# One load of query weights in two pieces, 16 partitions and then 112

## The chip, the core and the metric

The kernel runs on one core of a Trainium2 chip. The core has five engines with queues of their own: TensorE (PE, matmuls; its weight loads are listed as PEld), VectorE (DVE), ScalarE (ACT), GpSimd (POOL) and SyncE (SP, which here issues nearly all transfers). Sixteen DMA engines move data between the chip's memory (HBM) and the core's on-chip memory of 128 partitions. Engines and transfers tell each other by semaphores that work is done. The metric is the device time of one execution in microseconds (us).

## The reference

One token goes through attention over a cache of 65,536 positions and then a bilinear feed-forward block, all in fp32:

```
xn = layernorm(x)                              # x: 1 x 512
q  = xn @ wq                                   # 512 x 4096: 32 heads of 128, 4 for each of 8 cache heads
p  = softmax(q . k_cache / sqrt(128))          # k_cache, v_cache: 8 x 65536 x 128
h  = x + (p @ v_cache) @ wo
out = h + ((ln(h) @ w_gate) * (ln(h) @ w_up)) @ w_down     # F = 1792
```

The two caches are 537 MB of the 564.66 MB that the kernel reads.

## The kernel before

Everything large passes through two buffers, `kv[0]` and `kv[1]`, each 128 partitions x 16,384 fp32 (64 KiB for a partition, 8.39 MB in all). The host lays each operand out in blocks of that shape. The loads alternate between the buffers: first the query weights `wq` into `kv[1]` (line 118), then the first block of the cache into `kv[0]` (`even(0)`, line 142), then 63 more blocks (4 of keys, 4 of values for each of 8 heads), then `wo`, `gu` (gate and up weights) and `wd` (down weights), which are cut into two, three and six pieces. SP issues them all on one queue, in the order of the program. Before each load from the second cache block on, SP waits for the semaphore `free`, which VectorE raises when TensorE is done with the buffer. The input row `x` (`x_row`) is loaded from ACT's queue.

TensorE works on a block in 32 windows of 512 columns (`windows`, line 355), a matmul each, with the small operand `st` held as weights. It waits for the block's semaphore: `s_a0` for `kv[0]`, `s_b0` for `kv[1]`. A transfer raises its semaphore by 16 when all of it has landed, and a wait for 16 stands before the first window.

At the start, VectorE makes the layernorm of `x` (lines 168 to 180), TensorE turns it into columns (line 352), and VectorE copies these columns into `st` (line 209, `diagonal(0)`) and raises `qt`; with `qt` and `s_b0` TensorE starts the windows over `wq` (lines 434 to 437). When these are done (`kd`), VectorE raises `free`, and SP issues the second block of the cache. The tensor `q_all` that follows is used by all heads. The order on each queue is that of the code; nothing is rearranged.

Of the kernel before, what the change touches and what calls it, by code (L numbers as in the profile page):

```python
# [8 lines left out]
P = 128  # L9
D = 512  # L10
HKV, REP, DH = 8, 4, 128
SK = 65536
CK = 16384
NT = SK // CK
TPC = CK // P
KT = D // P
# [25 lines left out]
def body(nc, xr, kvd, wq, wo, gu, wd, out):  # L42
    pe_e, dve_e, act_e, pool_e, sp = nc.tensor, nc.vector, nc.scalar, nc.gpsimd, nc.sync

    def tile(name, *shape, align=32):
        return nc.alloc_sbuf_tensor(name, list(shape), F32, align_bytes=align).ap()
# [15 lines left out]
    kv = [tile(f"kv{i}", P, CK, align=1024) for i in range(2)]  # L62
# [22 lines left out]
    def sem(name):  # L85
        sems.append(nc.alloc_semaphore(name))
        return sems[-1]
# [8 lines left out]
    s_b0, s_b18, s_b28 = (sem(f"s_b{i}") for i in (0, 18, 28))  # L96
    s_wd = [sem(f"s_wd{i}") for i in WD_CUTS[:-1]]
    s_xr, s_wo = sem("s_xr"), sem("s_wo")
    late, s_act, s_pool, s_y, s_out = (sem(n) for n in ("late", "s_act", "s_pool", "s_y", "s_out"))
    wd_t = kv[0]  # L100
    end = 2 * HKV * NT

    def take(e, s, n=1):
        e.wait_ge(s, n).then_inc(s, -n)  # L104
# [10 lines left out]
    def odd(g):  # L115
        sp.dma_start(kv[1], kvd[g]).then_inc(s_b0, 16)

    sp.dma_start(kv[1], wq).then_inc(s_b0, 16)
    pe_e.br("pe_main")
    dve_e.br("dve_main")  # L120
    take(act_e, da)
# [74 lines left out]
    def diagonal(lo):  # L196
        return bass.AP(tensor=st.tensor, offset=33 * lo, ap=[list(st.ap[0]), [256, KT], [33, 8 - lo]])

    def spread(a, n):
        return a.unsqueeze(2).to_broadcast([P, KT, n])  # L200
# [5 lines left out]
        take(dve_e, pd)  # L206

    picked = ptp[0][:, 0:32].rearrange("p (b c) -> p b c", b=4)
    dve_e.tensor_copy(diagonal(0), spread(ps[0][:, 0:KT], 8)).then_inc(qt, 1)
    dve_e.sem_inc(tl, 1)  # L210
    take(dve_e, kd)
# [310 lines left out]
```

## Time and profile before

| | us |
|---|---|
| median of 3 runs | 1308.34 (1308.08 to 1308.45) |
| profiled execution, its own time | 1308.59 |
| its span, from the first to the last instruction | 1307.3 |
| TensorE busy in the span | 676.0 |
| VectorE busy | 102.9 |
| read from HBM | 564.66 MB |

The page gives busy times and, in 40 slices of the span, the busy share in tenths of each engine and of the 16 DMA engines. Views of the trace give the waits (who waited, for whom, how long in total, how often, the longest), the timeline (start, length, engine, line, operation, output <- inputs, count, and in brackets the idle time before and what ended it), windows (busy times, granted clock, DMA share and rate in a stretch) and the chain of waits that ended last. "SPq" is an issue by SP.

### The profile page before, as it was taken

The numbers are of one execution on the slowest core, as the hardware profiler recorded it, in microseconds if no ns is written. First come the engines' busy times: TensorE is split into PE (matmuls) and PEld (weight loads), VectorE is DVE, ScalarE is ACT, GpSimd is POOL, SyncE is SP. The second block draws the span as 40 slices with busy tenths as digits, with TensorE's granted clock in tenths as the row PEclk, the third lists the DMA queues.
The fourth block names the chain that finished last, engine by engine and source line by source line (L and its number), as shares of the span: only waits on it lengthen the run. The fifth ranks groups of instructions, "written<-read, shape, count | busy, mean of one in ns | idle before, by whom it ended". The sixth has DMA issues, their size and how long they took to land. (4 is left out here: it accounts for less than half of the span.)

```text
span 1307.3 us, 10815 instructions
## 1 busy us (share of the span) xinstructions
PE 676.0 (52%) x4606; PEld 187.8 (14%) x4606; DVE 102.9 (8%) x251; ACT 54.9 (4%) x106; POOL 4.2 (0%) x14
## 2 busy tenths in 40 slices
PE   3446445446535644554643654454563555355457
PEld 1112111111101111111110111111110111111112
DVE  2001010010000000000000101001000100000011
ACT  0000000000000000000000000000000000000000
POOL 1000000000000000000000000000000000000000
PEclk9676677677677767767667777867776776776779
DMA  9999999999999999999999999999999999999999
GB/s 417 417 449 417 449 417 449 417 449 419 447 435 431 439 427 449 417 449 417 449 417 449 417 449 419 447 435 431 441 425 449 417 449 417 449 417 449 417 433 387
DMA packets 11074, 564.72 MB, mean 432 GB/s; under 512 B 1233, under 2 KB 1345, under 8 KB 1858
## 3 DMA queue, kind: packets, MB, share of 16 engines
q1 hardware_dynamic: 11072, 564.72, 99.8%
q10 hardware_dynamic: 2, 0.00, 0.0%
HBM read 564.66 MB, written 0.06 MB: 432 GB/s over the span
## 5 line engine op out<-in xcount | busy, mean ns | idle before, releaser
L360 PE MATMUL ps<-kv,st 128*32 128x512 f32 x4308 | 620.2, 738 | 562.6 <-DMA kv<-in_kv 541.8
L360 PEld LDWEIGHTS ps<-kv,st 128*32 128x32 f32 x4308 | 150.0, 132 | 1016.5 <-DMA kv<-in_kv 586.1
L244 DVE TENSOR_REDUCE mx<-sc 128x1 f32<-128x512 f32 x32 | 22.0, 686 | 577.9 <-DVEq L104 577.9
L416 PE MATMUL ptp<-ident,ex 128*128 128x128 f32 x128 | 27.3, 371 | 19.8 <-ACT ex L226 19.5
L222 ACT COPY sc<-ps 128x512 f32<-128x512 f32 x32 | 18.7, 585 | 440.2 <-ACTq L104 440.1
L226 ACT ACTIVATE ex<-sc,nbias 128x512 f32<-128x512 f32 x32 | 22.8, 714 | 304.4 <-ACTq L104 304.4
L276 DVE TENSOR_TENSOR orow<-ps,orow 128x512 f32<-128x512 f32 x16 | 11.1, 692 | 261.6 <-DVEq L104 261.6
L222 ACT ACT_TABLE_LOAD x8 | 10.3, 1283 | 427.7 <-ACTq L104 427.7
L263 DVE COPY st<-ptp 128x512 f32<-128x512 f32 x32 | 22.1, 692 | 44.5 <-DVEq L104 44.5
L416 PEld LDWEIGHTS ptp<-ident,ex 128*128 128x128 f32 x128 | 20.2, 188 | 22.9 <-ACT ex L226 22.9
L409 PE MATMUL sm<-ident,m 128*1 128x128 f32 x16 | 4.5, 283 | 27.3 <-DVE m L246 17.6
L279 DVE TENSOR_TENSOR orow<-ps,orow 128x256 f32<-128x256 f32 x16 | 6.0, 420 | 138.5 <-DVEq L104 138.5
L274 DVE COPY orow<-ps 128x512 f32<-128x512 f32 x8 | 5.5, 692 | 101.7 <-DVEq L104 101.7
L411 PE MATMUL sm<-ones,mexp 1*128 1x1 f32 x32 | 6.9, 281 | 6.8 <-DVE mexp L253 6.8
L448 PE MATMUL ptp<-ident,orow 128*128 128x128 f32 x32 | 6.6, 293 | 3.0 <-DVE orow L279 3.0
L409 PEld LDWEIGHTS sm<-ident,m 128*1 128x1 f32 x16 | 1.3, 79 | 41.8 <-DVE m L246 24.9
L411 PEld LDWEIGHTS sm<-ones,mexp 1*128 1x128 f32 x32 | 5.5, 214 | 9.5 <-DVE mexp L253 8.5
L226 ACT ACTIVATION_READ_ACCUMULATOR ex<-sc,nbias 128x1 f32 x32 | 6.0, 186 | 0.0
L236 DVE COPY st<-qx 128x1024 f32<-128x1024 f32 x8 | 5.6, 694 | 1.2
L352 PE MATMUL ps<-ident,xn_row 1*128 1x1 f32 x4 | 0.6, 245 | 8.8 <-DVE xn_row L180 8.8
L205 DVE COPY gu_sb<-ps 128x256 f32<-128x256 f32 x4 | 1.5, 420 | 32.0 <-DVEq L104 32.0
L448 PEld LDWEIGHTS ptp<-ident,orow 128*128 128x128 f32 x32 | 3.2, 140 | 5.3 <-DVE orow L279 3.7
(78 smaller groups left out, 58.9 us busy)
## 6 DMA issues: line engine op xcount, KB each, us to landing
kv<-in_wo SPq DMA_DIRECT2D x1, 6144.0 KB, 24.2
kv<-in_gu SPq DMA_DIRECT2D x1, 3584.0 KB, 17.6
kv<-in_gu SPq DMA_DIRECT2D x1, 2560.0 KB, 23.3
kv<-in_wo SPq DMA_DIRECT2D x1, 2048.0 KB, 28.7
kv<-in_wd SPq DMA_DIRECT2D x2, 1024.0 KB, 15.4
kv<-in_kv SPq DMA_DIRECT2D x64, 29.0
kv<-in_gu SPq DMA_DIRECT2D x1, 1024.0 KB, 25.2
kv<-in_wd SPq DMA_DIRECT2D x2, 512.0 KB, 17.6
```

The source lines that it names most:

```text
L222: act_e.copy(sc[s], ps[s % 2]).then_inc(ad, 1)
L226: act_e.activation(ex[s - n], sc[s], AF.Exp, bias=nbias[:, 0:1], scale=SCALE, accum_out=sums[:, s:s + 1]).then_inc(atok[s - n], 1)
L236: dve_e.tensor_copy(st, qx.rearrange("p (g c) -> p g c", c=32)).then_inc(qt, 2)
L244: dve_e.tensor_reduce(out=mx[:, s:s + 1], in_=sc[s], axis=AX.X, op=ALU.max).then_inc(own, 1)
L263: dve_e.tensor_copy(st[:, :, 0:16].rearrange("p g (b h) -> p b g h", h=REP), ptp[n % 2].rearrange("p (b g h) -> p b g h", b=4, h=REP)).the ...
L276: mine(dve_e.tensor_tensor(out=orow, in0=ps[n % 2], in1=orow, op=ALU.add))
L279: dve_e.tensor_tensor(out=orow[:, cs], in0=ps[1][:, cs], in1=orow[:, cs], op=ALU.add).then_inc(tob, 1)
L360: i = mm(ps[buf][32 * j:32 * j + 32, :], st[:, 8 * j + r, :], kv[buf][:, w * 512:(w + 1) * 512], start=(r == 0), stop=(r in (1, 2, 7)), sk ...
L409: pe_e.transpose(sm[1][0:1, 0:P], m1, ident).then_inc(pd, 1)
L411: mm(sm[0][:, 0:1], mexp.rearrange("p g h -> p (g h)"), ones[0:1, 0:1], start=True, stop=True).then_inc(pd, 1)
L416: i = pe_e.transpose(ptp[half][:, b * P:(b + 1) * P], ex[half][:, b * P:(b + 1) * P], ident)
L448: i = pe_e.transpose(ptp[1][:, b * P:(b + 1) * P], orow[:, b * P:(b + 1) * P], ident)
```

## The change

The one load of `wq` becomes two. The first takes one row of 64 KiB into each of partitions 0 to 15 and has a semaphore of its own, `s_wq`. The second takes partitions 16 to 127 and raises `s_b0`, as the whole load did. The host lays the weights out as 16 pieces of 8 rows: the first row of piece e is that of partition e, the other seven are those of partitions 16+7e to 22+7e. The first load reads the first rows of the 16 pieces, the second the other seven of each. VectorE waits for `s_wq` before it copies the columns of the layernorm into `st`.

```
-    sp.dma_start(kv[1], wq).then_inc(s_b0, 16)
+    sp.dma_start(kv[1][0:16, :], wq[:, 0, :]).then_inc(s_wq, 16)
+    sp.dma_start(kv[1][16:P, :], wq[:, 1:8, :]).then_inc(s_b0, 16)
...
     picked = ptp[0][:, 0:32].rearrange("p (b c) -> p b c", b=4)
+    take(dve_e, s_wq, 16)
     dve_e.tensor_copy(diagonal(0), spread(ps[0][:, 0:KT], 8)).then_inc(qt, 1)
...
+    q = lay(A_wq, KT, P, HKV, 512, perm=(1, 2, 0, 3)).reshape(P, CK)
...
-        "wq": lay(A_wq, KT, P, HKV, 512, perm=(1, 2, 0, 3)).reshape(P, CK),
+        "wq": np.concatenate([q[0:16].reshape(16, 1, CK), q[16:P].reshape(16, 7, CK)], axis=1),
```

SP's queue at its start, before (`in_wq` and `in_kv` are the tensors in HBM; the sizes are partitions x elements):

```order
L118 DMA kv<-in_wq 128x16384
L113 DMA kv<-in_kv 128x16384
L143 UNCONDITIONAL_BRANCH
L116 ISA
L116 DMA kv<-in_kv 128x16384
```

and after:

```order
L118 DMA kv<-in_wq 16x16384
L119 DMA kv<-in_wq 112x1x16384
L113 DMA kv<-in_kv 128x16384
L144 UNCONDITIONAL_BRANCH
L116 ISA
L116 DMA kv<-in_kv 128x16384
```

The first cache block now stands third instead of second; nothing else of this queue moved.

VectorE's queue around the copy into `st`, with the semaphores that it waits for, before:

```order
L187 TENSOR_SCALAR neg_mean<-mean_m,sel 128x128 [waits own]
L191 COPY sel_pad<-sel 128x1 [waits pool]
L192 COPY acc<-x_row 1x512
L209 COPY st<-ps 128x4x8 [waits own,pd]
L205 COPY gu_sb<-ps 128x256 [waits kd]
```

and after:

```order
L188 TENSOR_SCALAR neg_mean<-mean_m,sel 128x128 [waits own]
L192 COPY sel_pad<-sel 128x1 [waits pool]
L193 COPY acc<-x_row 1x512
L211 COPY st<-ps 128x4x8 [waits own,pd,s_wq]
L206 COPY gu_sb<-ps 128x256 [waits kd]
```

The copy has one more wait, for the load of 16 partitions; its place is the same.

More of the change, by code (lines that the diff above doesn't have):

```diff
@@ L98, in body @@
     s_xr, s_wo = sem("s_xr"), sem("s_wo")
-    late, s_act, s_pool, s_y, s_out = (sem(n) for n in ("late", "s_act", "s_pool", "s_y", "s_out"))
+    late, s_act, s_pool, s_wq, s_y, s_out = (sem(n) for n in ("late", "s_act", "s_pool", "s_wq", "s_y", "s_out"))
     wd_t = kv[0]
```

## Prediction

> **What bounds the kernel now.** I read the page first, for the share of each engine and of the DMA engines.
>
> ```profile
> span 1307.3 us, 10815 instructions
> PE 676.0 (52%) x4606; PEld 187.8 (14%) x4606; DVE 102.9 (8%) x251; ACT 54.9 (4%) x106; POOL 4.2 (0%) x14
> DMA  9999999999999999999999999999999999999999
> DMA packets 11074, 564.72 MB, mean 432 GB/s; under 512 B 1233, under 2 KB 1345, under 8 KB 1858
> ```
>
> The busiest compute engine works for 52% of the span. The DMA engines are at 9 in all forty slices, the first and the last included: the transfer of 564.72 MB is the kernel. The tiny packets are worth a count. The program issues 77 transfers from SP (1 query weight, 64 cache, 2 `wo`, 3 `gu`, 6 `wd`, 1 output) and one small one from ACT; 77 x 16 + 1 = 1233, exactly the packets under 512 B. So each SP transfer ends with one tiny packet on each of 16 engines, also the output, which spans 112 partitions. I take from it that 112 partitions do not leave engines out.
>
> Next I asked who waits, and what the transfers do in each stretch.
>
> ```profile
> PE ps L360 <- DMA kv<-in_kv: 541.8, 64, 11.0
> PE ps L360 <- DMA kv<-in_wq: 13.3, 1, 13.3
> core 0: us, PE busy (x) PEld busy (x) DVE busy (x) ACT busy (x) POOL busy (x), PEclk, DMA share, GB/s
> 2.00:22.00 20.00, 0.58 (x4) 0.50 (x4) 5.53 (x13) 1.58 (x2) 3.00 (x8) 1.00 0.98 419
> ...
> 42.00:1260.00 1218.00, 627.28 (x4254) 172.65 (x4258) 88.62 (x200) 53.30 (x104) 0.00 (x0) 0.73 1.00 434
> 1285.00:1304.00 19.00, 14.69 (x116) 4.67 (x114) 3.04 (x16) 0.00 (x0) 0.00 (x0) 1.00 0.98 414
> ```
>
> TensorE waits for a cache load all 64 times, 8.5 us each on average. Over the long middle the DMA share is 1.00 at 434 GB/s, or 27.1 GB/s for each of 16 engines. No engine time is free there, so whatever engine time is lost at the start cannot be won back later. This holds as long as the next transfer always stands in the queue, which the timeline shows:
>
> ```profile
> 0.74 0.41 SPq L118 DMA_DIRECT2D kv<-in_wq  x1
> 1.21 0.42 SPq L113 DMA_DIRECT2D kv<-in_kv  x1
> 22.70 8.86 PE L360 MATMUL ps<-kv,st 128*32 128x512 f32 x64 [13.35 <-DMA kv<-in_wq]
> 32.05 0.34 SPq L116 DMA_DIRECT2D kv<-in_kv  x1
> 42.02 9.44 PE L360 MATMUL ps<-kv,st 128*32 128x512 f32 x64 [7.64 <-DMA kv<-in_kv]
> ...
> 1230.13 0.34 SPq L116 DMA_DIRECT2D kv<-in_kv  x1
> ```
>
> The load issued at 32.05 has 9.97 us of the load before it still ahead (TensorE gets that one at 42.02). From 32.05 to 1230.13 there are 62 steps of one load: 19.32 us each. A load is 128 rows of 64 KiB, one row for one partition; 8 rows for each engine, so a row takes an engine 19.32 / 8 = 2.416 us. The chain of waits ends with the last weights and a short tail:
>
> ```profile
> 1285.50 17.97 DMA kv<-in_wd
> 1303.47 0.04 issue
> ...
> 1305.31 0.29 DVE y L478
> ```
>
> The end is thus: start of the stream + engine time of the stream + a tail of some 4 us that the change does not touch.
>
> **The change part by part.**
>
> *The new transfer itself.* SP issues one more; the issue took 0.41 us in the row of line 118, so the second piece goes out at about 1.2 us and the first cache load at about 1.6 to 1.7. Engine time: 16 more tiny packets, one on each engine. The window from 1285 to 1304 holds most of the six `wd` transfers and still has a DMA share of 0.98, so all of its transfers together lost at most 0.02 x 19 = 0.4 us. I take 0 for the one more. What hides its issue and its latency is the first row of each engine, which runs at least 2.416 us: the second piece is due only when that row ends. In the present stream that is at about 22.70 - 7 x 2.416 = 5.8 us (less the time of the landing), against an issue at 1.2. If the cover were gone, the cost would be the time from an issue to its landing with nothing ahead in the queue:
>
> ```profile
> out_y<-y SPq DMA_DIRECT2D x1, 56.0 KB, 1.6
> ```
>
> So 0 to 1.6 us, and I take 0. [...]
>
> *A sooner start.* The query weights land 22.70 - 0.74 = 21.96 us after their issue, 8 x 2.416 = 19.33 of them rows; 2.63 us are start and landing. The small load of `x_row`, issued at the same 0.74, is there within 1.29 us:
>
> ```profile
> 0.74 0.51 ACTq L106 DMA_DIRECT2D x_row<-in_xr  x1
> 2.03 0.67 DVE L168 TENSOR_REDUCE ln_s<-x_row 1x1 f32<-1x512 f32 x1 [0.79 <-DMA x_row<-in_xr]
> 10.20 0.21 DVE L209 COPY st<-ps 128x32 f32<-128x32 f32 x1 [0.26 <-DVEq L104]
> ```
>
> If sixteen rows start as fast as that one, the gain is at most 2.63 - 1.29 = 1.3 us. I take 0; the bounds are -1.3 and 0.
>
> *VectorE's new wait.* It stands ahead of the copy of line 209, which ran at 10.20; behind it wait TensorE's first windows, which need the copy and the whole query weight (22.70 now). The first piece lands before the second, so even at 20 us this wait costs nothing.
>
> *The 16 partitions.* This is the term that decides. At any moment the 16 engines each write one row into one partition: 16 partitions take 434 GB/s, so a single partition can take 27.1 GB/s. Today an engine has eight rows of a load over 128 partitions; after the change, all 16 engines write partitions 0 to 15 at once. The trace does not show whether neighbouring partitions share a way into the memory. If each had its own, 16 rows take 2.416 us and nothing is lost. If the 434 GB/s come as 16 paths of 27.1, one for each eight partitions, and eight neighbours make one path, 16 partitions have two paths and take 8 x 2.416 = 19.33 us: 16.9 us lost on every engine. Between the ends lie 8 paths (2.4 lost) and 4 paths (7.25 lost). The nearest row is the load over 128 partitions, which shows full rate for a spread-out set only; for a set as narrow as this I choose the middle of the ends in doublings, towards the loss: 4 paths, 4 x 2.416 = 9.66 us for the first piece, 7.25 us lost on all engines.
>
> *The 112 partitions.* The host lays the source out as 16 pieces of seven rows, so I take it that engine e writes partitions 16+7e to 22+7e. At each step the sixteen engines stand seven partitions apart, instead of in the places of a whole load. With paths shared by neighbours, two engines then meet on one path in some steps, and such a step takes 4.83 us instead of 2.416. For the unluckiest engine between none and all seven steps double: 0 to 16.9 us. No row tells more; I take the middle, three and a half steps, 8.46 us. A load counts as landed only when its last engine is done, and the end of the kernel waits for the last engine too, so the unluckiest one counts. Engines that run ahead by up to 9.97 us still find the next load in the queue; beyond that they pause, which harms nobody.
>
> [...]
>
> *Sum.* 0 + 0 + 0 + 7.25 + 8.46 = 15.7 us. Against the profiled execution's 1308.59 us this makes 1324.3; that execution is 0.25 us above the median of the three runs, 1308.34, so the forecast is 1324.0 us.
>
> **The rivals.**
>
> *Not slower: every partition, or every pair of neighbours, has its own way.* Then both pieces run like a whole load; the place is the first 20 us and the price is between -1.3 and +1.6 us (or +2.4 with 8 paths and no meetings later): 1307.0 to 1310.7, at the middle about 1308.3. For it: 16 partitions do take the full 434 GB/s at every moment of the present stream. Against it: those are never known to be 16 neighbours. It decides from the point where the first piece has landed by 0.74 + 2.63 + 2.416 + 2.6 = 8.4 us.
>
> *Only the first piece is slow.* Seven partitions apart may be as good as the present places. Then 7.25 us are lost: 1315.6 us. For it: 112 of 128 partitions cover nearly all paths, whatever these are. Against it: each step writes only one partition for each engine.
>
> *Worse.* Two paths, or meetings in all seven steps, or three engines on a path: 24 us and more, 1332 us upwards. The count of tiny packets speaks against a worse case still, in which 112 partitions use fewer engines.
>
> **How the numbers follow.** What a measurement here can tell from no change is about 0.2%, 2.6 us. Chances: both pieces slow (forecast) 0.61; only the first 0.20; worse 0.05; neither 0.14, of which 0.01 is a gain of over 2.6 us, since the start offers 1.3 at most. So slower 0.86, same 0.13, faster 0.01. The forecast's own range is one and a half to six doubled steps (3.6 to 14.5 us) beside the 7.25: 1319 to 1330. The range reaches down to the case of the first piece alone with part of its loss (1312) and leaves out the 0.14 and the 0.05: 1312 to 1330.
>
> **What the changed profile would show.** TensorE's first windows start at about 38 us instead of 22.70, and the one wait for the query weights grows from 13.3 to about 29 us. The first piece lands about 12 us after its issue, and VectorE's copy of 10.20 moves to about 13. In the window from 2 to 22 the rate falls well below the present 419 GB/s; from the third load on the distance of two issues is 19.32 us as before, and the tail after the last landing is unchanged. The prediction is wrong if the first piece lands within 7 us of its issue, if the first windows start before 25 us, or if later loads change their distance.

## The result, and the profile after

The changed kernel takes 1329.23 us (median of five runs, 1328.45 to 1329.92) against 1308.34 (1308.0 to 1308.5) for the kernel before: a ratio of 1.016, 95% interval 1.0147 to 1.0172. It is slower by 20.9 us. The forecast was 1324.0, range 1312 to 1330, slower.

The head of the page:

```profile
span 1327.8 us, 10817 instructions
DMA  9999999999999999999999999999999999999998
GB/s 217 377 428 426 442 440 426 428 442 440 424 430 442 440 424 430 442 438 424 432 442 438 422 434 442 438 422 434 442 438 422 434 442 438 421 436 442 438 415 368
DMA packets 11090, 564.72 MB, mean 425 GB/s; under 512 B 1249, under 2 KB 1361, under 8 KB 1874
```

The DMA engines count as busy in all slices but the last, yet in the first slice of 33 us they move only 217 GB/s, and 377 in the second; after that the rates are the usual ones. A packet that waits in its engine counts as busy: in the window from 22 to 42 us below the share is 1.01 at 256 GB/s. The busy shares of the page would not have shown this loss; the rate does. (A window counts a packet where it starts. Fourteen of the first 16 rows start before 2.00, so the share of 0.72 and the 164 GB/s from 2 to 22 are without them.) The tiny packets went from 1233 to 1249, one more for each of 16 engines, so the piece of 112 partitions ran on all 16 engines.

The waits, the timeline of the start (the issues by SP, VectorE's copy, TensorE's first windows), and the windows:

```profile
PE ps L362 <- DMA kv<-in_kv: 541.8, 64, 11.0
PE ps L362 <- DMA kv<-in_wq: 34.8, 1, 34.8
```

```profile
0.74 0.39 SPq L118 DMA_DIRECT2D kv<-in_wq  x1
1.20 0.68 SPq L119 DMA_DIRECT2D kv<-in_wq  x1
1.92 0.58 SPq L113 DMA_DIRECT2D kv<-in_kv  x1
...
12.70 0.21 DVE L211 COPY st<-ps 128x32 f32<-128x32 f32 x1 [2.75 <-DVEq L104]
...
44.20 9.98 PE L362 MATMUL ps<-kv,st 128*32 128x512 f32 x64 [34.82 <-DMA kv<-in_wq]
63.40 8.93 PE L362 MATMUL ps<-kv,st 128*32 128x512 f32 x64 [6.41 <-DMA kv<-in_kv]
82.69 9.52 PE L362 MATMUL ps<-kv,st 128*32 128x512 f32 x64 [10.37 <-DMA kv<-in_kv]
```

```profile
core 0: us, PE busy (x) PEld busy (x) DVE busy (x) ACT busy (x) POOL busy (x), PEclk, DMA share, GB/s
2.00:22.00 20.00, 0.58 (x4) 0.50 (x4) 5.06 (x13) 1.58 (x2) 3.01 (x8) 1.00 0.72 164
22.00:42.00 20.00, 0.00 (x0) 0.00 (x0) 0.00 (x0) 0.00 (x0) 0.00 (x0) 1.00 1.01 256
62.00:1260.00 1198.00, 614.74 (x4186) 170.50 (x4186) 86.90 (x196) 53.34 (x104) 0.00 (x0) 0.73 1.00 434
```

The 64 waits for cache loads are the same 541.8 us to the tenth; the one for the query weights grew from 13.3 to 34.8. TensorE's first windows begin at 44.20 instead of 22.70, 21.5 us late, and the next two at distances of 19.20 and 19.29, a little under the 19.32 and 19.33 of before; from 62 us on the rate is 434 GB/s again. The first piece was there by 12.70, when VectorE's copy ran; the piece of 112 partitions took some 31 us after that. The chain of waits ends as before, 20.5 us later (1323.97 against 1303.47):

```profile
1305.92 18.04 DMA kv<-in_wd
1323.97 0.04 issue
```

So all of the loss lies in the load of the query weights, and the rest of the kernel wins only 1.0 us of it back.

### The profile page after: what moved, and what is told of

Its sections match the earlier page's. It is cut to its first block, busy times and chain, and to the rows that moved or that the text cites. A ratio compares the mean times of both kernels' runs of the same rounds, so it can differ in the third digit from the quotient of the medians.

```text
span 1327.8 us, 10817 instructions
## 1 busy us (share of the span) xinstructions
PE 673.9 (51%) x4606; PEld 188.1 (14%) x4606; DVE 102.3 (8%) x251; ACT 54.9 (4%) x106; POOL 4.2 (0%) x14
## 2 busy tenths in 40 slices
DMA packets 11090, 564.72 MB, mean 425 GB/s; under 512 B 1249, under 2 KB 1361, under 8 KB 1874
## 5 line engine op out<-in xcount | busy, mean ns | idle before, releaser
L362 PE MATMUL ps<-kv,st 128*32 128x512 f32 x4308 | 617.6, 736 | 584.3 <-DMA kv<-in_kv 541.8
```

Of the source, the lines that this page charges most:

```text
L362: i = mm(ps[buf][32 * j:32 * j + 32, :], st[:, 8 * j + r, :], kv[buf][:, w * 512:(w + 1) * 512], start=(r == 0), stop=(r in (1, 2, 7)), sk ...
```

## The experiments

Theory A: groups of neighbouring partitions share a path into the on-chip memory, sixteen paths for 128 partitions; two engines on one path each get less. A1 and A2 differ in what happens to the engines that have a path to themselves: by A1 a shared path holds them up too, by A2 only the engines on the shared path are late. Rivals: C, the order of the rows in HBM; E, the new transfer and its wait. Each experiment is compared with the kernel before on the same chip; the median of before was 1308.32 to 1308.44 in all of them.

### The host's order undone

```
-    sp.dma_start(kv[1][0:16, :], wq[:, 0, :]).then_inc(s_wq, 16)
-    sp.dma_start(kv[1][16:P, :], wq[:, 1:8, :]).then_inc(s_b0, 16)
+    sp.dma_start(kv[1][0:16, :], wq[0:16, :]).then_inc(s_wq, 16)
+    sp.dma_start(kv[1][16:P, :], wq[16:P, :]).then_inc(s_b0, 16)
...
+        "wq": q,
```

> The same two pieces (partitions 0 to 15, then 16 to 127), but the host leaves the rows of the query weights in their plain order, so the sixteen engines read rows 64 KiB apart in the first piece and 448 KiB apart in the second, instead of 512 KiB apart. Theory A (the destination: neighbouring partitions share write paths): nothing changes, 1328 to 1330 us, first windows at about 44 us. Rival C (the source: rows read 512 KiB apart in HBM are slow): the loss goes, 1308 to 1312 us, first windows at 23 to 26 us.

Measured: 1329.45 us (1328.95 to 1330.1), ratio 1.0161 (1.0144 to 1.0178), the same as the changed kernel. From its timeline:

```profile
12.89 0.21 DVE L211 COPY st<-ps 128x32 f32<-128x32 f32 x1 [4.22 <-DVEq L104]
...
45.08 8.48 PE L362 MATMUL ps<-kv,st 128*32 128x512 f32 x64 [37.00 <-DMA kv<-in_wq]
```

Both pieces land within 0.9 us of when they did with the host's order, and the time is the same. Rival C falls: the order of the rows in HBM is not what costs the 20.9 us.

### Two pieces over all partitions

```
+    sp.dma_start(kv[1][:, 0:2048], wq[:, 0:2048]).then_inc(s_wq, 16)
+    sp.dma_start(kv[1][:, 2048:CK], wq[:, 2048:CK]).then_inc(s_b0, 16)
...
+        "wq": q,
```

> Two pieces again, with the same two semaphores and the same wait on VectorE, but each over all 128 partitions: columns 0 to 2047 first, then the other 14,336. Theory A: the loss goes, since every engine keeps its own path: 1308.0 to 1309.0 us. Rival E (one more transfer, its issue and the added wait cost the time): it stays near 1329 us, or at least 1310 if the wait alone costs 2 us.

Measured: 1308.46 us (1308.01 to 1308.83, ten runs), ratio 1.0001 (0.9991 to 1.0010). The issues and TensorE's first windows:

```profile
kv<-in_wq SPq DMA_DIRECT2D x1, 7168.0 KB, 21.3
...
kv<-in_wq SPq DMA_DIRECT2D x1, 1024.0 KB, 4.9
```

```profile
22.58 8.80 PE L362 MATMUL ps<-kv,st 128*32 128x512 f32 x64 [13.22 <-DMA kv<-in_wq]
```

A first piece of 1 MiB, as many bytes as in the change, lands 4.9 us after its issue when it goes to 128 partitions, and the second transfer, the second semaphore and VectorE's wait cost nothing that the interval can tell (it is 1.3 us wide on either side). Rival E falls. The landing at 4.9 us is also what a first piece without any sharing would have done (5.05 by the prediction's terms), against some 12 us in the change.

### Eight pieces: which 16 partitions

Three kernels load the query weights, in plain order, as eight pieces of 16 partitions each. They differ only in which 16: neighbours, every eighth, or every fourth of one half. VectorE's wait, left out below, is for the first seven pieces.

```
+    parts = [(16 * j, 16 * j + 16, 1) for j in range(8)]               # neighbours
+    parts = [(j, P, 8) for j in range(8)]                              # every eighth
+    parts = [(h + j, h + 64, 4) for h in (0, 64) for j in range(4)]    # every fourth
+    for n, (lo, hi, step) in enumerate(parts):
+        sp.dma_start(kv[1][lo:hi:step, :], wq[lo:hi:step, :]).then_inc(s_b0 if n == len(parts) - 1 else s_wq, 16)
```

> The load of the query weights as eight pieces of 16 neighbouring partitions each, plain order in HBM. Theory A with four paths for 16 neighbours: each piece takes 4 x 2.416 = 9.66 us, 77.3 us instead of 19.3, so +58 us: about 1366 us. With two paths (eight neighbours to a path): 8 x 19.3 us, +135 us: about 1443. Rival C: no rows 512 KiB apart here, 1308 to 1312 us. Rival E (a cost for each transfer): seven more transfers at 20.9 us each, about 1455 us.

> Eight pieces of 16 partitions each, now every eighth partition (0, 8, ..., 120), then 1, 9, ... and so on; the number of transfers and their bytes are those of the kernel with eight pieces of neighbours. [...] If a path is eight neighbours: sixteen paths, no loss, about 1308.5. Rival E: as with neighbours. Rival C: rows 512 KiB apart in every piece, +20 us or more.

> Eight pieces of 16 partitions, every fourth partition of one half (0, 4, ..., 60; 1, 5, ..., 61; and so on; then the same from 64). No two are in one group of four neighbours. [...] If each group of four has a path of its own among those at work, no loss: about 1308.5 us.

| 16 partitions | median us | ratio (95%) | over before | one piece |
|---|---|---|---|---|
| neighbours | 1362.63 | 1.0415 (1.0398 to 1.0433) | 54.3 | (19.33 + 54.3) / 8 = 9.20 us |
| every eighth | 1329.19 | 1.016 (1.014 to 1.0181) | 20.8 | 5.02 us |
| every fourth of a half | 1328.84 | 1.0156 (1.0139 to 1.0173) | 20.5 | 4.98 us |

(One of the four executions with every eighth partition took 3194.74 us and is left out of its row; the other three lie between 1329.0 and 1329.23. Its cause is open.) The rates from 12 to 32 us, of neighbours, every eighth and every fourth:

```profile
12.00:32.00 20.00, 0.00 (x0) 0.00 (x0) 0.00 (x0) 0.00 (x0) 0.00 (x0) 1.00 0.94 105
```

```profile
12.00:32.00 20.00, 0.00 (x0) 0.00 (x0) 0.00 (x0) 0.00 (x0) 0.00 (x0) 1.00 0.98 203
```

```profile
12.00:32.00 20.00, 0.00 (x0) 0.00 (x0) 0.00 (x0) 0.00 (x0) 0.00 (x0) 1.00 1.01 210
```

The same bytes in the same number of transfers take 9.2 or 5.0 us a piece, depending on the partitions. (The rows read in HBM move with them, and rival C too gave some 20 us for every eighth partition; but the first piece of the change read rows 512 KiB apart and the one in plain order rows 64 KiB apart, and both were equally slow.) 105 GB/s is as much as four paths of 27.1 GB/s carry (108), 203 to 210 as much as eight (217). Every eighth partition would have been free if eight neighbours made a path; it is not, and every fourth of a half is no better (4.98 us a piece). So in theory A partitions that are no neighbours share a path too; which of them do is not shown.

### Sixteen partitions seven apart

```
+    parts = [(j, 112, 7) for j in range(7)] + [(112, P, 1)]
```

> Seven pieces of 16 partitions seven apart (0, 7, ..., 105; 1, 8, ...; up to 6, 13, ..., 111), then partitions 112 to 127. [...] Theory A1 (a shared path holds up all 16 engines): these steps take what the seven steps of the second piece took, some 13 us over 16.9, and the last piece 7.25 over 2.416: about 1329 us. [...]

Measured: 1329.66 us (1329.06 to 1330.36), ratio 1.0164 (1.0147 to 1.0181). Rate while the seven pieces run:

```profile
2.00:32.00 30.00, 0.58 (x4) 0.49 (x4) 5.31 (x12) 1.58 (x2) 3.00 (x8) 1.00 1.20 271
12.00:32.00 20.00, 0.00 (x0) 0.00 (x0) 0.00 (x0) 0.00 (x0) 0.00 (x0) 1.00 1.12 249
```

A1 said about 1329 us. (The first window is somewhat high, since the first 16 rows all start in it.) The changed kernel has the same 249 GB/s from 12 to 32 us. The pieces spell out, one by one, sets like those that the load of 112 was taken to go through, each 16 partitions lower, and they cost as much (21.3 us over the kernel before, against 20.9). How many of the 16 engines meet in each set is not shown, so this run alone does not tell A1 from A2.

### Extra transfers on eight engines

Two kernels put three transfers of eight rows ahead of an otherwise unchanged start; they go to the other buffer, and SP issues the first cache block, which overwrites them, when they have landed. Each of the three runs on eight engines: the packets under 512 B are 1257 instead of 1233, eight more for each.

```
+    for lo, hi, step in ((1, 32, 4), (2, 32, 4), (3, 32, 4)):          # spread
+    for lo, hi, step in ((0, 8, 1), (8, 16, 1), (16, 24, 1)):          # neighbours
+        sp.dma_start(kv[0][lo:hi:step, :], wq[lo:hi:step, :]).then_inc(s_wq, 16)
     sp.dma_start(kv[1], wq).then_inc(s_b0, 16)
+    take(sp, s_wq, 48)
```

> The kernel before with three more transfers ahead of the query weights, each of eight rows of 64 KiB into eight partitions four apart (1, 5, ..., 29, then from 2, then from 3) of the other buffer, which the first cache block overwrites once they have landed. [...] Theory A: three rows more on these engines, 3 x 2.416 = 7.25 us, about 1315.6 us, and the rate from 2 to 22 us stays near 420 GB/s. If a narrow set of partitions is slow in itself, whatever its spread: two to four times as much, 1323 to 1337 us.

> The same as the kernel with three extra transfers, but into eight neighbours each (0 to 7, 8 to 15, 16 to 23): four engines on each of two paths. [...] Theory A: 3 x 9.66 = 29.0 us for the eight engines, about 1337 us. A1 (a shared path holds up all engines): the other eight are slowed too, some 110 to 180 GB/s from 2 to 22 us. A2 (only those on the shared path): the other eight run at full rate, about 270 GB/s in that window.

Measured: spread 1316.44 us, ratio 1.0062 (1.0045 to 1.0078), 8.1 us more than before; neighbours 1334.88, ratio 1.0202 (1.0185 to 1.0219), 26.6 us more, somewhat under the 29.0 expected. The window from 2 to 22 us of the spread kernel, and of the one with neighbours:

```profile
2.00:22.00 20.00, 0.58 (x4) 0.50 (x4) 5.46 (x13) 1.58 (x2) 3.01 (x8) 1.00 0.94 393
```

```profile
2.00:22.00 20.00, 0.58 (x4) 0.50 (x4) 5.52 (x13) 1.58 (x2) 3.01 (x8) 1.00 1.13 134
```

Eight partitions at a time are not slow in themselves: four apart, three rows cost 8.1 us, 0.9 more than the 7.25 that they take with a path for each (the rate, 393, is a little under the 420 expected). It also narrows down what shares: eight partitions four apart among 0 to 31 are nearly at full rate, sixteen four apart in one half at half of it (210 GB/s), so the meetings there come with the wider set; which partitions meet is not shown. With neighbours, a row of the eight engines takes as long as one of 16 neighbours does (9.12 to 9.15 us below, against 9.20 a piece), as with four engines on a path; so by theory A eight engines crowd on two paths, and the other eight are meanwhile at the query weights. If those had run at their 27.1 GB/s on paths of their own, the window would show 8 x 27.1 + 2 x 27.1 = 271 GB/s. It shows 134. So engines on free paths are slowed too: A1.

The trace also keeps a record of every row of 64 KiB (its start and its length, without its engine), and the rows say the same. In the kernel with neighbours the second row of all 16 engines, crowded or free, took 9.12 to 9.15 us. The free engines' third rows took 8.21 to 8.45, and their fourth, which start at 30.07, after the last extra rows, 2.42. Which paths the other eight stood on is not shown. But in the kernel before, the rows of the same load take 2.42 us on all 16 engines from the second row on, so no two of these engines meet on a path, and at most two of the eight can have stood on the two crowded ones; six would not, and none was fast.

### Two extra transfers of 16 rows

Two extra transfers of 16 rows instead, into partitions seven apart, from 3 and 4 in one kernel (called the kernel with one pair) and from 0 and 1 in the other. Each transfer of the first was taken to have one pair of engines on a shared path, each of the second two pairs; no run before these two showed that.

```
+    for lo, hi, step in ((3, 109, 7), (4, 110, 7)):     # from 3 and 4
+    for lo, hi, step in ((0, 106, 7), (1, 107, 7)):     # from 0 and 1
```

> The kernel before with two more transfers ahead of the query weights, each of 16 rows of 64 KiB into 16 partitions seven apart (3, 10, ..., 108 and 4, 11, ..., 109) of the other buffer, which the first cache block overwrites later. [...] Without any sharing two rows cost 2 x 2.416 = 4.8 us. If one shared path makes all 16 engines take twice as long, and no more paths matter: 2 x 4.83 = 9.7 us, 1318.0 us, the same as with two pairs. If the hold-up grows with the number of shared paths: less than with two pairs, 6 to 7.5 us, 1314.5 to 1315.8 us.

> [...] If one shared path already doubles the time of all engines: 9.7 us, 1318.0 us, equal to the kernel with one pair. If the hold-up grows with the number of shared paths: 9 to 10 us here, 1317.3 to 1318.5 us, and 2 to 3 us less with one pair.

Measured: from 3 and 4 1316.13 us (1315.85 to 1316.61), ratio 1.0059 (1.0042 to 1.0076); from 0 and 1 1317.48 (1317.37 to 1317.73), ratio 1.0069 (1.0052 to 1.0086). Over before that is 7.7 and 9.0 us, where two rows without sharing would take 4.83. The second came out at the 9 to 10 us expected for a hold-up that grows; the first missed its 6 to 7.5 us and lies only 1.35 us below the second, less than the 2 to 3 expected. The engines of a pair alone would lose up to 2 x 2.416 us here, so these totals cannot separate A1 from A2. The single rows can. In the second of the extra transfers from 3 and 4, two rows take 4.71 and 5.17 us, as one pair on a path would, and the other fourteen 2.99 to 3.55, more than 2.42 and less than twice that. So the free engines lose part of a row beside one pair: it neither leaves them alone nor stops everybody for twice as long. In the second transfer from 0 and 1 the rows of all 16 engines take 4.72 to 4.83 us; how many pairs meet in it is not shown.

## Why the prediction was right, and where its size was off

- **The bound.** Right: what the engines lost in the first 44 us came out at the end, 21.5 us at the first windows and 20.5 at the last landing. The 1.0 us between them is won back over the first cache loads: TensorE's fifth set of windows starts 21.0 us late (121.25 against 100.23). "Cannot be won back" was thus right but for this 1.0; why the latest engines catch up a little is open.
- **The new transfer, its wait, the sooner start: 0.** Right: the two pieces over all partitions give 1.0001 (0.9991 to 1.0010). SP's second and third issue took 0.68 and 0.58 us in the changed kernel, hidden as said.
- **The 16 partitions: 7.25 us, four paths.** Right: VectorE's copy came at 12.70 (forecast about 13). The eight pieces of neighbours give 9.20 us for one such piece, so 6.8 lost, and their 105 GB/s is about what four paths of 27.1 carry. That it was four and not two, eight or sixteen was a choice of the middle; no row of the kernel before told it, so hitting it was in part luck.
- **The 112 partitions: 8.46 us.** This term was mis-sized. It measured 20.9 - 6.8 = 14.1 us (with the 6.8 of the eight pieces), 5.8 doubled steps of seven instead of three and a half; 1329.23 lies in the range, but only 0.8 us under its upper end. The step that failed is the assumption that only the engines that meet on a path are late, while the others run ahead, so that a meeting hurts whoever has it. The rows of the changed kernel show it: in the third and the fourth step of the piece two rows took 4.40 to 4.74 us, and the other fourteen 2.92 to 3.65, where engines that run ahead would take 2.42. The run with neighbours beside other engines shows the same (134 GB/s instead of 271): a shared path holds up the engines that are not on it, so a step with a meeting counts for everybody. These two steps are also why it was 14.1 and not the 16.9 of seven doubled steps; in the second and the last three all 16 rows took 4.08 to 4.88. (The first, 4.81 to 5.91, begins while the first piece still runs.) How many engines meet in a step is not shown, so how much of the 14.1 is hold-up and how much is meetings in more than half of the steps stays open. The 16 engines end the piece between 40.88 and 44.16 us, all of them far later than the 22.05 to 22.66 of before.
- **The rivals.** "Only the first piece is slow" failed at 14.1 us; "not slower" failed at the first piece. Of "worse", one condition came true as far as the rows tell, a loss in all seven steps (no row under 2.92 us), but not its price of 24 us and more: two of the steps do not double for everybody. First windows at 44.20 instead of about 38, and the wait of 34.8 instead of 29, are the same 6 us of the second term.

Where in the chip the free engines are held, on the way out of HBM or on the way into the partitions, is not shown. No version tried beats the kernel before; the best, two pieces over all partitions, is equal to it.

## What to carry to other kernels

When the DMA engines are the bound, a load should give all sixteen of them the whole 128 partitions; to get something early, cut by columns, not by partitions (here 1308.46 us against 1329.23). A cut by partitions can slow all engines while it lasts, so look at the rows of every engine, not only of those that meet: here, while two of sixteen rows took 4.40 to 4.74 us, the other fourteen took 2.92 to 3.65 instead of 2.42, and in other steps all of them took 4.08 to 4.88. Look at the rate in a short window rather than at the busy share: here the engines were "busy" (1.01) at 256 GB/s instead of 434.

## What the runs showed of the hardware

- 16 neighbouring partitions take 105 GB/s, 16 partitions eight apart or, in one half, four apart 203 to 210, 128 partitions 434. A row of 64 KiB takes an engine 2.42 us in a load of 128 partitions; a piece of 16 rows takes 9.20 us with neighbours and about 5.0 with the other two sets.
- Partitions that are no neighbours slow each other too: every fourth partition of a half is as slow as every eighth of the whole, 4.98 and 5.02 us a piece, while every fourth of the first 32 is nearly at full rate (8.1 us for three rows, 7.25 with a path for each). Which partitions share a path is not shown beyond this.
- Unexpected: while eight engines write neighbours, the other eight lose their rate too, 134 GB/s in all instead of 271; their rows take 9.12 to 9.15 us like those of the crowded eight. Where two rows of 16 took 4.71 and 5.17 us, the other fourteen took 2.99 to 3.55.
